# Scores of a split-precision attention: three products on 64 rows of a head, two heads side by side, where four on 128 rows stood

## The chip, the cores and the metric

The kernel runs on one core of a Trainium2 chip (trn2). The metric is the device time of one execution in microseconds (us), the median of several runs. TensorE (PE) multiplies, with weight loads (PEld) as instructions of their own; VectorE (DVE), ScalarE (ACT) and GpSimd (POOL) work on rows of 128 partitions; SyncE (SP) issues nearly all DMAs.

## The reference

Attention over 8 batches of 8 heads, with queries averaged in pairs, and then a feed-forward part over all tokens (float32, head dimension 64, 1152 keys, 576 pooled queries a head):

```python
q_pool = q.reshape(B, H, S // factor, factor, D).mean(axis=3)      # B, H, S, D = 8, 8, 1152, 64; factor 2
scores = scale * np.matmul(q_pool, k.transpose(0, 1, 3, 2))
scores = scores - np.max(scores, axis=-1, keepdims=True)
attn = np.exp(scores)
attn = attn / (np.sum(attn, axis=-1, keepdims=True) + 1e-09)
out = np.matmul(attn, v)                                           # heads side by side make x: 4608 x 512
h = np.maximum(np.maximum(x @ w1, x @ w2), x @ w3)                 # 4608 x 768
return h @ w_out                                                   # 4608 x 512
```

## The kernel before, in words

Two heads make a pair, whose 2 x 64 head dimensions fill the 128 partitions. The attention runs in 64 turns `d`, each for one pair and one half of its queries (288 columns, `QH`). In a turn there are nine blocks `kk` of 128 keys. For each block PE writes the scores of both heads into one of two PSUM slots (`pqk`, a bank for each head), ACT copies them to SBUF (`s`, L664), and DVE keeps the running maximum (`acc`, L670 and L673). A slot is free for the block after next when both have read it. Then comes the maximum over all keys: DVE folds (L714), PE turns (L724), DVE and ACT take a high and a low part, POOL spreads them (`diag`, L739), PE makes them wide (L790). DVE subtracts (L809), ACT takes the exponential (L815), POOL adds the keys up (`ksum`, L846 and L848), PE multiplies by the values (`pav`, L875) and totals the sums (L891), and the quotient becomes `xr` (L902), split into `xh` and `xl` for the feed-forward part. That part (`ffn`) is done in chunks of up to 512 tokens, three products for each product of two split operands (L1165 and L1221), and its matmuls stand between those of the attention on PE.

The first pairs (`n < PLAIN`, `plain_heads`) take the scores in plain float32: L642, one matmul a head on 64 rows, the two heads at rows 0 and 64 of the array. A matmul in plain float32 is two records in the trace. The other pairs (`heads`) use numbers of type float32r: q and k are cut into a high part (a cast on ACT, L528 and L535) and a low part (a subtraction on POOL, L532 and L539), in tiles `qraw` and `kraw`. Then DMAs on SP (`move_q` L573, `move_k` L565) put the parts where 128 rows of one head hold both: `kc` has the high part of k on rows 0 to 63 and the low part on rows 64 to 127, and `qq` has each part of q twice. Four matmuls of 128 rows make a block: for each head one with the high part of q (L654) and one with its low part (L655).

The order of all work is written out: `ORDER` lists the steps of the plan by number, and every engine and every DMA queue works them off in that order. `mode`, `cols` and the times in the steps were for the program that made the list; at run time they do nothing.

Of the kernel before, what the change touches and what calls it, by code (L numbers as in the profile page):

```python
# [8 lines left out]
F32 = mybir.dt.float32  # L9
# [10 lines left out]
NK = 9  # L20
# [301 lines left out]
THIRDS = 7  # L322
LENT = 4
SUMS = range(8)
SPLIT = 8
AHEAD = {3: 5, 4: 5, 5: 5, 6: 5, 7: 5}
GIFT = {0: 1, 1: 2, 2: 3, 3: 3, 4: 1}
PLAIN = 10
APART = 0

class Step:
    def __init__(self, plan, engines, fn, after, **kw):
# [970 lines left out]
```

## Time and profile before

| | |
|---|---|
| time, median of 3 runs (lowest to highest) | 1349.48 us (1347.28 to 1354.3) |
| span of the profiled execution, first to last instruction | 1345.0 us |
| TensorE clock granted over the span, share of full | 0.999 |
| busy share of the span: PE, PEld, DVE, ACT, POOL | 98%, 77%, 75%, 68%, 83% |
| matmul records | 8544 |

The time of the profiled execution by itself is not given beside its span; the span lies 4.5 us under the median of the runs. PE's busy share counts a matmul from its start to its end, and matmuls overlap, so the starts of successive matmuls tell the pace, not the durations. The last 145 us are feed-forward work alone, with the other engines nearly idle.

### The profile page before, as it was taken

What the parts mean: (1) busy time and instruction counts of PE and PEld (TensorE: products, weight loads), DVE (VectorE), ACT (ScalarE), POOL (GpSimd) and SP (SyncE); (2) the same over time, 40 slices, a digit from 0 to 9 for tenths busy, and PEclk for the clock granted to TensorE, in tenths of its full rate; (3) what the DMA queues carried; (4) which work ended last, traced back from release to release, by engine and by line L of the source; (5) the groups of instructions that cost most, each with busy time, mean ns of one, the idle gap of its engine ahead of it and who ended that gap; (6) DMA issues with size and microseconds to landing.
All of it is one profiled execution on the core that took longest, in us unless ns stands there. A gap on an engine that the chain in (4) does not pass through costs nothing.

```text
span 1345.0 us, 24149 instructions
## 1 busy us (share of the span) xinstructions
PE 1322.0 (98%) x8544; PEld 1029.4 (77%) x8544; DVE 1015.1 (75%) x1351; ACT 907.9 (68%) x1547; POOL 1123.0 (83%) x895
## 2 busy tenths in 40 slices
PE   7999999999999999999999999999999999999999
PEld 3455668887777877777777877777777877779998
DVE  7889987888779878887888888878888888842110
ACT  6998886776667766786677766776767766652211
POOL 3797899999899999999899999898999998865310
PEclk9999999999999999999999999999999999999999
DMA  6677787875676467547676557656675576527341
GB/s 220 236 266 244 250 243 236 242 239 161 173 214 177 127 191 230 153 136 213 175 217 184 154 150 222 167 162 194 167 201 159 164 201 172 159 71 227 133 160 49
DMA packets 112296, 250.11 MB, mean 186 GB/s; under 512 B 14512, under 2 KB 68272, under 8 KB 112176
## 3 DMA queue, kind: packets, MB, share of 16 engines
q1 hardware_dynamic: 112176, 248.57, 62.6%
q8 instruction: 68, 1.11, 0.4%
q14 instruction: 52, 0.43, 0.1%
HBM read 168.30 MB, written 18.87 MB: 139 GB/s over the span
## 4 chain that ended last, share of the span: by engine, by line
PE 83%; POOL 5%; DVE 4%; DMA 4%; issue 2%; ACT 2%; SPq 0%; ACTq 0%; POOLq 0%; DVEq 0%
PE ff L1165 31%; PE pav L875 16%; PE ff L1221 10%; PE pqk L654 8%; PE pqk L655 8%; PE pqk L642 3%; POOL ksum L848 3%; PE ff L891 2%; PE ff L875 2%; DMA kc<-kraw 2%; DVE acc L673 2%; PE bank_a L790 1%; PE ff L924 1%; DMA w<-w_split 1%; ACT s L664 1%
## 5 line engine op out<-in xcount | busy, mean ns | idle before, releaser
L848 POOL TENSOR_TENSOR ksum<-ksum,s 128x576 f32<-128x576 f32 x407 | 580.7, 1427 | 26.5 <-ACT s L815 8.8
L1165 PE MATMUL ff<-xh,w 128*128 128x512 f32 (+2 forms) x1584 | 470.3, 355 | 2.0 <-DMA w<-w_split 1.7
L664 ACT COPY s<-pqk 128x576 f32<-128x576 f32 x576 | 359.7, 641 | 142.3 <-PE pqk L655 100.3
L673 DVE TENSOR_TENSOR acc<-acc,pqk 128x576 f32<-128x576 f32 x448 | 334.7, 747 | 62.0 <-ACT s L664 52.3
L815 ACT ACTIVATE s<-s 128x864 f32<-128x864 f32 x384 | 348.0, 931 | 18.1 <-DVE s L809 17.2
L1165 PEld LDWEIGHTS ff<-xh,w 128*128 128x128 f32 x1584 | 283.9, 188 | 38.6 <-issue 4.5
L1165 PE MATMUL ff<-xl,w 128*128 128x512 f32 (+2 forms) x792 | 279.7, 353 | 0.0
L654 PE MATMUL pqk<-qq,kc 128*128 128x288 f32 x936 | 263.5, 300 | 4.4 <-DVE acc L673 1.2
L655 PE MATMUL pqk<-qq,kc 128*128 128x288 f32 x936 | 259.5, 295 | 0.0
L875 PE MATMUL pav<-s,v 128*64 128x288 f32 x2016 | 254.6, 407 | 0.0
L809 DVE TENSOR_TENSOR s<-s,bank_a 128x864 f32<-128x864 f32 x192 | 199.0, 1047 | 45.1 <-PE bank_a L790 38.0
L875 PEld LDWEIGHTS pav<-s,v 128*64 128x64 f32 x2016 | 144.2, 137 | 98.9 <-PE pqk L655 1.5
L654 PEld LDWEIGHTS pqk<-qq,kc 128*128 128x128 f32 x936 | 175.7, 188 | 30.0 <-DVE acc L673 8.9
L809 DVE TENSOR_TENSOR s<-s,pmb 128x864 f32<-128x864 f32 x182 | 188.8, 1045 | 1.2 <-PE pmb L790 1.0
L655 PEld LDWEIGHTS pqk<-qq,kc 128*128 128x128 f32 x936 | 176.0, 188 | 10.6
L1221 PE MATMUL ff<-h,wo 128*128 128x512 f32 (+2 forms) x792 | 162.7, 352 | 0.0
L1165 PEld LDWEIGHTS ff<-xl,w 128*128 128x128 f32 x792 | 148.9, 188 | 9.4
L1186 DVE TENSOR_TENSOR hm<-hm,ff 128x512 f32<-128x512 f32 (+2 forms) x132 | 76.3, 578 | 101.9 <-PE ff L1165 97.9
L1221 PEld LDWEIGHTS ff<-h,wo 128*128 128x128 f32 x792 | 129.0, 188 | 13.6 <-issue 0.9
L1197 POOL TENSOR_TENSOR h<-hm,h 128x512 fp32r<-128x512 f32 (+2 forms) x66 | 71.8, 1088 | 71.9 <-ACT h L1194 71.7
L899 DVE RECIPROCAL rs<-rs 128x288 f32<-128x288 f32 (+1 forms) x64 | 110.6, 1728 | 9.6 <-ACT rs L895 7.8
L846 POOL TENSOR_TENSOR ksum<-s 128x576 f32<-128x576 f32 x61 | 87.5, 1435 | 23.0 <-ACT s L815 22.6
(70 smaller groups left out, 1228.9 us busy)
## 6 DMA issues: line engine op xcount, KB each, us to landing
w<-w_split SPq DMA_DIRECT2D x180, 512.0 KB, 4.7
kc<-kraw SPq DMA_DIRECT2D x312, 96.0 KB, 3.6
qq<-qraw SPq DMA_DIRECT2D x208, 144.0 KB, 3.9
v<-in_vr_dram SPq DMA_DIRECT2D x36, 576.0 KB, 5.5
qraw<-in_qT_dram SPq DMA_DIRECT2D x26, 576.0 KB, 4.3
kraw<-in_kT_dram SPq DMA_DIRECT2D x26, 576.0 KB, 5.0
w<-in_win_dram SPq DMA_DIRECT2D x18, 512.0 KB, 4.3
w_split<-wo SPq DMA_DIRECT2D x18, 512.0 KB, 6.9
```

The source lines that it names most:

```text
L654: nc.tensor.matmul(ps[:, h - hs[0], :QH], w, qq[:, 0, h], start=True, stop=False)
L655: nc.tensor.matmul(ps[:, h - hs[0], :QH], w, qq[:, 1, h], start=False, stop=True)
L664: nc.scalar.copy(o.s[kk // 3][:, kk % 3, slice(*hs)], o.ps[kk, hs][:, :, :QH])
L673: nc.vector.tensor_tensor(acc, acc, ps, op=ALU.max)
L809: nc.vector.tensor_tensor(s, s, o.pb[h][:, None, :w].broadcast_to([P, 3, w]), op=ALU.subtract)
L815: nc.scalar.activation(s, s, AF.Exp, scale=SCALE)
L846: vec[e].tensor_tensor(o.ksum, o.s[0][:, 0], x, op=ALU.add)
L848: vec[e].tensor_tensor(o.ksum, o.ksum, x, op=ALU.add)
L875: nc.tensor.matmul(o.pav[64 * h : 64 * h + 64, :QH], pr.v[:, kk, h], o.s[kk // 3][:, kk % 3, h], start=(kk == 0), stop=(kk == NK - 1),)
L899: nc.vector.reciprocal(o.rs, o.rs)
L1165: nc.tensor.matmul(t.ps[:, : hi - lo], w[:, a, kk], xx[:, kk, lo:hi], start=(kk == 0 and i == 0), stop=(kk == 3 and i == 2),)
L1221: nc.tensor.matmul(t.ps[:, : hi - lo], ww[:, kk, ms], hh[kk // 3][:, kk % 3, lo:hi], start=(kk == 0 and i == 0), stop=(kk == 5 and i == 2),)
```

## The change

Pairs from `n = 8` on (`PLAIN` was 10) are split, 28 pairs in place of 26. The parts of q and k stay on the rows on which they were loaded: ACT casts the high part straight into `qq` and `kc`, POOL subtracts the low part into them, in pieces of 288 and 384 columns, and the DMAs `move_q` and `move_k` are gone. A block of scores is now six matmuls: high x high, high x low, low x high (the product of the two low parts is left out), each for both heads, one head on rows 0 to 63 and one on rows 64 to 127 of the array. `qq` is half as large and has three buffers (`QBUFS`). `ORDER` is made anew.

```diff
-PLAIN = 10
+PLAIN = 8
+QBUFS = 3
...
-        def k_high(e, x, y):
-            nc.scalar.copy(o.hl[:, 0, x:y].bitcast(F32R), o.hl[:, 1, x:y])
-        def k_low(e, x, y):
-            lo = o.hl[:, 1, x:y]
-            vec[e].tensor_tensor(lo.bitcast(F32R), lo, o.hl[:, 0, x:y], op=ALU.subtract)
...
-        def move_k(e, c, h, part):
...
-            nc.sync.dma_start(
-                o.kc[c][64 * part : 64 * part + 64, h].bitcast(F32),
-                o.hl[64 * h : 64 * h + 64, part, KC * c : KC * c + KC],
-            )
...
+        def q_high(e, half):
+            o.qq[half] = qpool.tile([P, 2, QH], F32R, tag="qq", name=f"qq{n}_{half}")
+            nc.scalar.copy(o.qq[half][:, 0], o.qr[:, 1, QH * half : QH * half + QH])
+        def q_low(e, half):
+            src = o.qr[:, 1, QH * half : QH * half + QH]
+            nc.gpsimd.tensor_tensor(o.qq[half][:, 1], src, o.qq[half][:, 0], op=ALU.subtract)
+        def k_high(e, c):
+            o.kc[c] = kpool.tile([P, 2, KC], F32R, tag="kc", name=f"kc{n}_{c}")
+            nc.scalar.copy(o.kc[c][:, 0], o.kr[:, KC * c : KC * c + KC])
+        def k_low(e, c):
+            src = o.kr[:, KC * c : KC * c + KC]
+            nc.gpsimd.tensor_tensor(o.kc[c][:, 1], src, o.kc[c][:, 0], op=ALU.subtract)
...
                     kc, qq = pr.kc[kk // 3], pr.qq[o.half]
-                    for h in range(*hs):
-                        w = kc[:, h, kk % 3 * P : kk % 3 * P + P]
-                        nc.tensor.matmul(ps[:, h - hs[0], :QH], w, qq[:, 0, h], start=True, stop=False)
-                        nc.tensor.matmul(ps[:, h - hs[0], :QH], w, qq[:, 1, h], start=False, stop=True)
+                    for i, (x, y) in enumerate(((0, 0), (0, 1), (1, 0))):
+                        for h in range(2):
+                            r = slice(64 * h, 64 * h + 64)
+                            nc.tensor.matmul(
+                                ps[:, h, :QH],
+                                kc[r, x, kk % 3 * P : kk % 3 * P + P],
+                                qq[r, y],
+                                start=i == 0,
+                                stop=i == 2,
+                                tile_position=(64 * h, 0),
+                            )
```

In the changed kernel the lines have other numbers: the six score matmuls are L582, the feed-forward ones L1099 and L1155, the values L809, `diag` made wide L724, the low parts of k and q L524 and L516 on POOL, and the key sums L782.

How the order moves is shown at two places. The first is PE in turn 33, behind the values of turn 32 (`pav32`), where the scores of pair 21 begin. Before, two blocks of scores go straight on to the widening of turn 33's maximum (`bank_a`, L790) and to feed-forward work:

```order
L875 MATMUL pav32_6030<-s32_2_5780,v20_5532 64x288 x6
L654 MATMUL pqk1_127<-qq21_0_5818,kc21_1_5918 128x288
L655 MATMUL pqk1_127<-qq21_0_5818,kc21_1_5918 128x288
L654 MATMUL pqk1_127<-qq21_0_5818,kc21_1_5918 128x288
L655 MATMUL pqk1_127<-qq21_0_5818,kc21_1_5918 128x288
L654 MATMUL pqk0_126<-qq21_0_5818,kc21_1_5918 128x288
L655 MATMUL pqk0_126<-qq21_0_5818,kc21_1_5918 128x288
L654 MATMUL pqk0_126<-qq21_0_5818,kc21_1_5918 128x288
L655 MATMUL pqk0_126<-qq21_0_5818,kc21_1_5918 128x288
L790 MATMUL bank_a_94<-diag1_116,wide_108 128x288
L1165 MATMUL ff0_130<-xh_120,w0_122 128x512
```

The changed kernel at the same place, with two blocks of six, then six feed-forward matmuls, the first widening, and the next block:

```order
L809 MATMUL pav32_6424<-s32_2_6147,v20_6324 64x288 x6
L582 MATMUL pqk0_126<-qq21_0_6306,kc21_0_6313 128x288 x6
L582 MATMUL pqk1_127<-qq21_0_6306,kc21_1_6369 128x288 x6
L1099 MATMUL ff1_131<-xh_120,w0_122 128x512
L1099 MATMUL ff1_131<-xl_121,w0_122 128x512
L1099 MATMUL ff1_131<-xh_120,w0_122 128x512 x2
L1099 MATMUL ff1_131<-xl_121,w0_122 128x512
L1099 MATMUL ff1_131<-xh_120,w0_122 128x512
L724 MATMUL pmb33_1_6487<-diag1_116,wide_108 128x288
L582 MATMUL pqk0_126<-qq21_0_6306,kc21_1_6369 128x288 x6
```

The scores keep coming two blocks at a time between values and feed-forward work, but each such group is now of another tile shape than what stands on either side of it. Over the whole order PE goes from one tile shape (128 rows x 128 columns, 64 x 128, 128 x 64 and the like) to another 260 times before and 695 times now.

The second place is POOL, where the low parts of pair 21 are made. Before, one instruction of 1152 columns makes the low part of k, between the key sums of turns 30 and 31 (that of q, in 576 columns, stands four rows above this piece):

```order
L848 TENSOR_TENSOR ksum30_5616<-ksum30_5616,s30_2_5419 128x576
L1017 TENSOR_TENSOR xl_121<-xr_119,xh_120 128x96
L848 TENSOR_TENSOR ksum30_5616<-ksum30_5616,s30_2_5419 128x576 x2
L539 TENSOR_TENSOR kraw21_5650<-kraw21_5650 128x1152
L846 TENSOR_TENSOR ksum31_5830<-s31_0_5469 128x576
L1017 TENSOR_TENSOR xl_121<-xr_119,xh_120 128x128
L739 TENSOR_TENSOR diag0_115<-pick_110,parts0_113 64x576
```

In the changed kernel the pieces of k and q stand apart, here among the sums of turn 32, on both sides of `diag`:

```order
L524 TENSOR_TENSOR kc21_1_6369<-kraw21_6310,kc21_1_6369 128x384
L836 TENSOR_TENSOR xr_119<-xr_119,rs31_6420 128x288
L951 TENSOR_TENSOR xl_121<-xr_119,xh_120 128x96
L951 TENSOR_TENSOR xl_121<-xr_119,xh_120 128x128
L673 TENSOR_TENSOR diag1_116<-pick_110,parts1_114 64x576
L524 TENSOR_TENSOR kc21_2_6471<-kraw21_6310,kc21_2_6471 128x384
L782 TENSOR_TENSOR ksum32_6380<-ksum32_6380,s32_1_6097 128x576
L516 TENSOR_TENSOR qq21_1_6316<-qraw21_6103,qq21_1_6316 128x288
```

The low parts moved later by about a turn, no DMA stands between them and PE any more, and POOL has five instructions for a pair's low parts where it had two.

## Rows read from the trace of the kernel before

**Rows 1.** The page: span, busy time by engine, and the chain that ended last.

```profile
span 1345.0 us, 24149 instructions
PE 1322.0 (98%) x8544; PEld 1029.4 (77%) x8544; DVE 1015.1 (75%) x1351; ACT 907.9 (68%) x1547; POOL 1123.0 (83%) x895
PE 83%; POOL 5%; DVE 4%; DMA 4%; issue 2%; ACT 2%; SPq 0%; ACTq 0%; POOLq 0%; DVEq 0%
```

**Rows 2.** PE's waits from 205 us to the end: us in total, times, longest.

```profile
PE pqk L654 <- DVE acc L673: 1.2, 2, 0.6
PE pqk L654 <- DMA kc<-kraw: 1.2, 2, 0.6
```

**Rows 3.** By stage: us; busy us of PE, PEld, DVE, ACT, POOL; clock; DMA share.

```profile
100.00:205.00 105.00, 102.83 (x773) 67.65 (x763) 95.34 (x144) 89.68 (x152) 91.39 (x77) 1.00 0.79 244
700.00:800.00 100.00, 100.00 (x622) 77.69 (x619) 81.60 (x102) 71.11 (x124) 96.96 (x79) 1.00 0.59 168
205.00:1125.00 920.00, 915.66 (x5758) 722.68 (x5757) 753.97 (x956) 653.97 (x1100) 857.50 (x667) 1.00 0.66 186
```

**Rows 4.** Groups by line and shape: count, then busy us and mean ns.

```profile
L654 PE MATMUL pqk<-qq,kc 128*128 128x288 f32 x936 | 263.5, 300 | 4.4 <-DVE acc L673 1.2 <-DMA kc<-kraw 1.2 <-DMA w<-w_split 1.1
```

**Rows 5.** PE's timeline, two blocks of split scores: start us, us, instruction.

```profile
608.00 0.29 PE L654 MATMUL pqk<-qq,kc 128*128 128x288 f32 x1
608.12 0.29 PE L655 MATMUL pqk<-qq,kc 128*128 128x288 f32 x1
...
608.91 0.30 PE L655 MATMUL pqk<-qq,kc 128*128 128x288 f32 x1
```

**Rows 6.** Timelines: four plain score matmuls, and four of their weight loads.

```profile
64.91 0.65 PE L642 MATMUL pqk<-qq,kc 64*128 64x288 f32 x4
...
60.25 0.30 PEld L642 LDWEIGHTS pqk<-qq,kc 64*128 64x128 f32 x4 [0.51 <-DVE acc L673]
```

**Rows 7.** PE's timeline where the tile shape changes, one way and back.

```profile
139.75 0.29 PE L1165 MATMUL ff<-xh,w 128*128 128x288 f32 x1
139.98 0.51 PE L642 MATMUL pqk<-qq,kc 64*128 64x288 f32 x2
...
173.68 0.65 PE L642 MATMUL pqk<-qq,kc 64*128 64x288 f32 x4
174.26 0.40 PE L1165 MATMUL ff<-xh,w 128*128 128x288 f32 x1
```

**Rows 8.** Groups by line and shape on POOL and ACT, columns as in rows 4.

```profile
L539 POOL TENSOR_TENSOR kraw<-kraw 128x1152 fp32r<-128x1152 f32 x26 | 69.9, 2688 | 7.2 <-DMA w<-w_split 3.3 <-ACT kraw L535 2.8 <-DMA qraw<-in_qT_dram 1.1
L532 POOL TENSOR_TENSOR qraw<-qraw 128x576 fp32r<-128x576 f32 x26 | 37.1, 1425 | 1.5 <-ACT qraw L528 1.3 <-DMA v<-in_vr_dram 0.2
L1197 POOL TENSOR_TENSOR h<-hm,h 128x288 fp32r<-128x288 f32 x24 | 19.4, 808 | 55.3 <-ACT h L1194 55.3
L528 ACT CAST qraw<-qraw 128x576 fp32r<-128x576 f32 x26 | 17.6, 676 | 1.7 <-POOL qraw L525 1.6
L1197 POOL TENSOR_TENSOR h<-hm,h 128x384 fp32r<-128x384 f32 x6 | 6.1, 1009 | 8.3 <-ACT h L1194 8.2
```

**Rows 9.** DMA issues: name, queue, count, KB each, median us to landing.

```profile
kc<-kraw SPq DMA_DIRECT2D x312, 96.0 KB, 3.6
qq<-qraw SPq DMA_DIRECT2D x208, 144.0 KB, 3.9
```

**Rows 10.** Groups by line: the two readers of a score slot.

```profile
L664 ACT COPY s<-pqk 128x576 f32<-128x576 f32 x576 | 359.7, 641 | 142.3 <-PE pqk L655 100.3 <-PE pqk L642 17.4 <-POOL ksum L848 8.6
L673 DVE TENSOR_TENSOR acc<-acc,pqk 128x576 f32<-128x576 f32 x448 | 334.7, 747 | 62.0 <-ACT s L664 52.3
```

**Rows 11.** PE's timeline: one plain score pair, then key sums, four tiles side by side.

```profile
61.67 0.41 PE L642 MATMUL pqk<-qq,kc 64*128 64x288 f32 x2
62.01 2.62 PE L924 MATMUL ff<-s,ones 128*32 128x288 f32 x36
```

**Rows 12.** POOL's `diag`, one a turn, in the long stage: busy us (count).

```profile
205.00:1125.00 920.00, 56.39 (x49) 1.00 0.66 186
```

More of the change, by code (lines that the diff above doesn't have):

```diff
@@ L382, in tile_attention_ffn @@
     kpool = ctx.enter_context(tc.tile_pool(name="kpool", bufs=4))
-    qpool = ctx.enter_context(tc.tile_pool(name="qpool", bufs=2))
+    qpool = ctx.enter_context(tc.tile_pool(name="qpool", bufs=QBUFS))
     vpool = ctx.enter_context(tc.tile_pool(name="vpool", bufs=2))
@@ L465, in load_q @@
         def load_q(e, half):
-            o.q[half] = qpool.tile([P, 2, 2, QH], F32R, tag="qq", name=f"qq{n}_{half}")[:, :, 0].bitcast(F32)
+            o.q[half] = qpool.tile([P, 2, QH], F32R, tag="qq", name=f"qq{n}_{half}").bitcast(F32)
             nc.sync.dma_start(o.q[half], qT[b, j, :, :, QH * half : QH * half + QH])
@@ L477, in plain_heads @@
         for i, (d, half) in enumerate(todo):
-            x = step("load", d, [("sp", 0.5)], lambda e, half=half: load_q(e, half), [qk.get((d - 2, NK - 1))], size=288)
+            x = step("load", d, [("sp", 0.5)], lambda e, half=half: load_q(e, half), [qk.get((d - QBUFS, NK - 1))], size=288)
             o.qready[half] = [step("prep", d, [dve(QH) if d == 0 else pool(QH)], lambda e, half=half: qsum(e, half), [x])]
@@ L504, in heads, with load_k, load_q @@
             before = None
-        first = n == 0
-        kparts = [(KC * c, KC * c + KC) for c in range(3)] if first else [(0, NK * P)]
-        qparts = [(0, QH), (QH, NQ)] if first else [(0, NQ)]
-        def load_k(e, x, y):
-            if x == 0:
-                o.hl = raw.tile([P, 2, NK * P], F32, tag="kraw", name=f"kraw{n}")
-            nc.sync.dma_start(o.hl[:, 1, x:y], kT[b, j, :, x:y])
-        def load_q(e, x, y):
-            if x == 0:
-                o.q = raw.tile([P, 2, NQ], F32, tag="qraw", name=f"qraw{n}")
-            nc.sync.dma_start(o.q[:, :, x:y], qT[b, j, :, :, x:y])
+        def load_k(e):
+            o.kr = raw.tile([P, NK * P], F32, tag="kraw", name=f"kraw{n}")
+            nc.sync.dma_start(o.kr, kT[b, j])
+        def load_q(e):
+            o.qr = raw.tile([P, 2, NQ], F32, tag="qraw", name=f"qraw{n}")
+            nc.sync.dma_start(o.qr, qT[b, j])
         def load_v(e):
@@ L521, in load_v @@
             nc.sync.dma_start(o.v, v[b, j])
-        def qsum(e, x, y):
-            lo = o.q[:, 1, x:y]
-            vec[e].tensor_tensor(lo, o.q[:, 0, x:y], lo, op=ALU.add)
-        def q_high(e, x, y):
-            nc.scalar.copy(o.q[:, 0, x:y].bitcast(F32R), o.q[:, 1, x:y])
-        def q_low(e, x, y):
-            lo = o.q[:, 1, x:y]
-            vec[e].tensor_tensor(lo.bitcast(F32R), lo, o.q[:, 0, x:y], op=ALU.subtract)
-        def k_high(e, x, y):
-            nc.scalar.copy(o.hl[:, 0, x:y].bitcast(F32R), o.hl[:, 1, x:y])
@@ L537, in k_low @@
-        def k_low(e, x, y):
-            lo = o.hl[:, 1, x:y]
-            vec[e].tensor_tensor(lo.bitcast(F32R), lo, o.hl[:, 0, x:y], op=ALU.subtract)
-        def pieces(key, at, engines, fn, parts, after, size=0):
-            return [
-                step(key, at + 0.01 * i, engines(y - x), lambda e, x=x, y=y: fn(e, x, y), a, size=(y - x) * size)
-                for i, ((x, y), a) in enumerate(zip(parts, after))
-            ]
-        work = (lambda m: [dve(m)]) if first else (lambda m: [pool(m)])
@@ L548, in heads @@
-        cast = lambda m: [("act", 0.09 + m / 1200)]
-        sp = lambda m: [("sp", 0.5)]
-        lq = pieces("load", r, sp, load_q, qparts, [before.qmoved if before else []] * len(qparts), size=1)
-        lk = pieces("load", r, sp, load_k, kparts, [before.kmoved if before else []] * len(kparts), size=0.5)
-        x = pieces("prep", r, work, qsum, qparts, [[a] for a in lq])
-        x = pieces("prep", r, cast, q_high, qparts, [[a] for a in x])
-        qs = pieces("prep", r, work, q_low, qparts, [[a] for a in x])
@@ L555, in heads @@
-        x = pieces("prep", r, cast, k_high, kparts, [[a] for a in lk])
-        ks = pieces("prep", r, work, k_low, kparts, [[a] for a in x])
-        o.kc, o.qq = {}, {}
-        o.kready, o.qready, o.kmoved, o.qmoved = {}, {}, [], []
-        def move_k(e, c, h, part):
-            if c not in o.kc:
-                o.kc[c] = kpool.tile([P, 2, KC], F32R, tag="kc", name=f"kc{n}_{c}")
-            nc.sync.dma_start(
-                o.kc[c][64 * part : 64 * part + 64, h].bitcast(F32),
-                o.hl[64 * h : 64 * h + 64, part, KC * c : KC * c + KC],
-            )
@@ L570, in move_q @@
-        def move_q(e, half, h, to):
-            if half not in o.qq:
-                o.qq[half] = qpool.tile([P, 2, 2, QH], F32R, tag="qq", name=f"qq{n}_{half}")
-            (nc.scalar if e == "act" else nc.sync).dma_start(
-                o.qq[half][64 * to : 64 * to + 64, :, h].bitcast(F32),
-                o.q[64 * h : 64 * h + 64, :, QH * half : QH * half + QH],
-            )
-        for d, half in todo:
-            o.qready[half] = [
-                step(
-                    "move",
-                    d,
-                    [("act" if first and half == 0 else "sp", 0.6)],
-                    lambda e, half=half, h=h, to=to: move_q(e, half, h, to),
-                    [qs[half % len(qs)], qk.get((d - 2, NK - 1))],
-                    size=144,
-                )
-                for h in range(2)
-                for to in range(2)
-            ]
-            o.qmoved += o.qready[half]
-            if d == r:
-                for c in range(3):
-                    gone = qk[kuse[-4]] if len(kuse) > 3 else None
-                    kuse.append((o.last, 3 * c + 2))
-                    o.kready[c] = [
-                        step(
-                            "move",
-                            r + 0.1 * (c + 1),
-                            [("sp", 0.6)],
-                            lambda e, c=c, h=h, part=part: move_k(e, c, h, part),
-                            [ks[c % len(ks)], gone],
-                            size=96,
-                        )
-                        for h in range(2)
-                        for part in range(2)
-                    ]
-                    o.kmoved += o.kready[c]
@@ L609, in heads, with qsum @@
-        o.lv = step(
-            "load",
-            r + 2,
-            sp(0),
-            load_v,
-            [av[pairs[n - 2].last]] if n > 1 else [] if n else o.qready[0] + o.kmoved,
-            size=576,
-        )
+        def qsum(e):
+            nc.gpsimd.tensor_tensor(o.qr[:, 1], o.qr[:, 0], o.qr[:, 1], op=ALU.add)
+        o.kc, o.qq = {}, {}
+        o.kready, o.qready = {}, {}
+        def q_high(e, half):
+            o.qq[half] = qpool.tile([P, 2, QH], F32R, tag="qq", name=f"qq{n}_{half}")
+            nc.scalar.copy(o.qq[half][:, 0], o.qr[:, 1, QH * half : QH * half + QH])
@@ new lines, in heads @@
+        cast = lambda m: [("act", 0.09 + m / 1200)]
+        lq = step("load", r, [("sp", 0.5)], load_q, before.qsplit if before else [], size=576)
+        lk = step("load", r, [("sp", 0.5)], load_k, before.ksplit if before else [], size=576)
+        sq = step("prep", r, [pool(NQ)], qsum, [lq])
+        o.qsplit, o.ksplit = [], []
+        for d, half in todo:
+            gone = [qk.get((d - QBUFS, NK - 1))]
+            x = step("prep", d, cast(QH), lambda e, half=half: q_high(e, half), [sq] + gone)
+            y = step("prep", d, [pool(QH)], lambda e, half=half: q_low(e, half), [x])
+            o.qready[half] = [x, y]
+            o.qsplit += [x, y]
@@ L619, in tile_attention_ffn @@
+        for c in range(3):
+            gone = qk[kuse[-4]] if len(kuse) > 3 else None
+            kuse.append((o.last, 3 * c + 2))
+            x = step("prep", r, cast(KC), lambda e, c=c: k_high(e, c), [lk, gone])
+            y = step("prep", r, [pool(KC)], lambda e, c=c: k_low(e, c), [x])
+            o.kready[c] = [x, y]
+            o.ksplit += [x, y]
+        o.lv = step("load", r + 2, [("sp", 0.5)], load_v, [av[pairs[n - 2].last]], size=576)
     blanks = step("top", max(TURN - 4, 0), [("dve", 3.2)], lambda e: blank(), [])
@@ L679, in scores @@
                     r,
-                    [pe(250 * n if pr.plain else 266 * n)],
+                    [pe(250 * n if pr.plain else 200 * n)],
                     product,
@@ L683, in scores @@
                     cols=576 * n,
-                    mode=3 if pr.plain else 0,
+                    mode=3,
                     take="ff" if apart else None,
```

545 rows, old and new, of the table ORDER are left out of this document.

## The prediction

> **What bounds the kernel now.** I read the page first: PE is busy for 98% of the span and has 83% of the chain that ended last, POOL 83% of the span and 5% of the chain [rows 1]. Then PE's waits: from 205 us to the end no line of them is over 1.2 us [rows 2], so PE is fed all the time, and what counts there is how closely its instructions follow each other. Then the stages, since a mean over the span hides the second engine: from 205 to 1125 us PE is busy for 915.7 of 920 us, and POOL for 857.5, which is 93.2%; its best stretch of 100 us has 96.96, with PE still at 100.00 [rows 3]. DVE (82%) and ACT (71%) have room there [rows 3]. The reader is to see that PE decides, and that POOL stands close behind it, where the span's 83% does not show it.
>
> **The sum on PE.** Durations of matmuls overlap, so I take starts.
>
> Removed: 1872 matmuls of split scores, 468 blocks of four (L654 has 936 [rows 4], L655 as many). In a run of eight the first starts at 608.00 and the last at 608.91 [rows 5]: 0.91 / 7 = 0.130 us each, and 1872 x 0.130 = 243.4 us. Pairs 8 and 9 leave the plain form: 2 pairs x 2 turns x 9 = 36 blocks. A plain block is two records for each head. Four records, which is one block, take 0.65 us from the first start to the last end [rows 6], and two side by side take 0.41 [rows 11]; so a pair of heads follows the other after 0.24 us, a block costs 0.48, and 36 of them 17.3 us.
>
> Added: 28 pairs x 2 turns x 9 = 504 blocks of three pairs of matmuls, one matmul for each head, 1512 in all. No float32r matmul on 64 rows is in the trace. From below, the plain pair needs 0.24 us for two passes over the same 288 columns, so one pass is 0.12; from above, two matmuls one behind the other take 0.26. I take 0.130, the pace of one float32r matmul of 288 columns, because the plain records show that two heads on 64 rows share their time: two take 0.41, which is barely longer than the 0.40 of one [rows 7, 11]. 1512 x 0.130 = 196.6 us (181 at the lower end, 393 at the upper). Issue is no obstacle: 36 matmuls and their 36 loads pass in 2.62 us [rows 11], at most 36 ns for each instruction, and a pair of scores needs four in 130 ns.
>
> Moved: the scores now have another tile shape than the feed-forward matmuls around them. In the trace that is not free. From L1165 to L642 the starts are 139.75 and 139.98, 0.23 apart in place of 0.13; on the way back the second pair of the run starts at 173.68 + 0.24 = 173.92 and L1165 at 174.26, 0.34 later in place of 0.24 [rows 7]. Each change of shape costs about 0.10 from rounded starts; I take 0.095. The order has 695 changes in place of 260, 435 more, and 435 x 0.095 = 41.3 us. Ends: 0.09 and 0.10 (39 to 44 us).
>
> Together: -243.4 - 17.3 + 196.6 + 41.3 = -22.8 us. Of the 64 us that the products save, the shape changes take back two thirds.
>
> **The term for POOL.** The low parts cost a pair 2.688 + 1.425 = 4.11 us now; in pieces they cost 3 x 1.009 + 2 x 0.808 = 4.64 (rows of the same shapes and types in the feed-forward part) [rows 8], so 0.53 more. Pairs 8 and 9 bring 4.64 us and a sum of about 1.43 in place of two of 0.81, 4.5 us each on POOL, in the stage from 100 to 205 us, where it has 91.4 of 105 busy [rows 3]; that fits into its gaps. In the long stage there are 49 turns [rows 12], 24.5 pairs and 441 blocks: PE loses 441 x 0.130 = 57.3 us, gets 49/56 of the 435 changes, 381 x 0.095 = 36.2, and needs 920 - 21.1 = 899 us. POOL needs 857.5 + 24.5 x 0.53 = 870.5, which is 96.8% of 899. That is what it reached in its best 100 us, and it would have to hold it for the whole stage. Between the mean of 93.2% and the best of 96.96% I take 96%, nearer to the best, since PE did not wait in that stretch: 870.5 / 0.96 = 907 us, 8 us over what PE needs. What is late then is `diag`, which stands in POOL's order among key sums and low parts; PE's widening of the maximum waits for it, and with it all feed-forward matmuls behind it, and next DVE's subtractions and ACT's exponentials.
>
> **What I cost at nothing.** The 520 DMAs for `kc` and `qq` go [rows 9], and SP's queue is free for the weights sooner; PE's waits for `kc` in the long stage were 1.2 us [rows 2], so little can be gained, and at most a few us in all. The wait of the scores is now on POOL and ACT themselves, without 3.6 to 3.9 us of landing [rows 9], and the order uses that up by making the low parts about a turn later; if POOL is late by more than what is left, the score matmuls stop and the feed-forward ones queued behind them too. ACT has three casts more a pair, each shorter than the 0.676 us of a cast of 576 columns [rows 8]: under 2 us a pair beside some 11 us of idle time (266 us in the stage [rows 3] over 24.5 pairs). Without that cover, the copy of 0.641 us and the maximum of 0.747 [rows 10] would let go of a score slot later and PE would wait for it. Both orders put two blocks side by side and then other work, so the slots are asked for no more often than before. The third buffer of `qq` only lets its casts go earlier.
>
> **A rule that speaks against it.** Two score matmuls share their time only if their weight loads do. Four loads on 64 rows take 0.30 us from the first start to the last end [rows 6]; at the 0.130 us at which loads and matmuls of the whole array follow each other [rows 5], the fourth would not even start before 0.39. So they do overlap. The Trainium skill, TensorE: Matmul & The Clock Gate, section LDWEIGHTS, says that a load is priced by its columns and not by its rows, 128 / 1.2 GHz = 107 ns for these. An estimate by that page, with the six loads of a block one behind the other: 504 x 6 x 0.107 = 323 us in place of 197, and about 1455 us in all. Four loads in 0.30 us speak against that reading.
>
> **The rivals.**
> - *POOL holds the pace.* If it is busy for no more than 93.2% of the stage, as now, the stage takes 870.5 / 0.932 = 934 us, 35 over PE's 899, and the kernel 1349.5 - 22.8 + 35 = 1362 us: slower. It decides from 94.2% down, where the stage takes 924 and the gain is gone. For it: POOL's idle time is spread over waits that come from the loop of maximum, `diag` and exponential, and some of that stays however late POOL is. Against it: the stretch at 96.96%.
> - *POOL keeps up, and a pair goes at less than 0.130.* With no POOL term 1349.5 - 22.8 = 1327; with 0.12 a pair another 15 us less, 1312, but then POOL would have to be busy for over 98% of the stage, which no stretch shows.
> - *The heads do not go side by side in float32r* (the change does not do what it says): six matmuls, or six loads, one behind the other at 0.130 make 393 us in place of 197, and 1327 + 197 = 1524. The plain records speak against it, but they are of another type.
>
> **How the numbers follow.** The span of the profiled execution is 1345.0 us [rows 1], 4.5 under the median of the runs; I leave that difference as it is. 1349.5 - 22.8 + 8 = 1334.7, rounded to 1335 us. Chances: this forecast (1325 to 1343) 0.54; POOL no hindrance or a faster pair (1310 to 1325) 0.17; POOL holding back (1343 to 1362) 0.20, of it three quarters within half a per cent of now; heads one behind the other 0.05; something else that costs, such as an order that fits badly, 0.04. Half a per cent, 1342.7 to 1356, is about what a measurement of this kernel can tell. So faster 0.72, same 0.15, slower 0.13. The range of 1312 to 1354 leaves out the serial case, the worst of POOL and the tip of the fast case.
>
> **What would show it.** Score matmuls in pairs that start a few ns apart, pair after pair 0.13 us later; 0.22 to 0.24 us from a feed-forward matmul of 288 columns to the first score; POOL at 95 to 97% of the long stage; PE's waits on `diag` and on the low parts some 10 us where they were near nothing. I am wrong if pairs start 0.26 apart, if a change of shape costs twice or nothing between float32r matmuls, or if POOL's busy share stays at 93% and PE waits for it.

## The result: slower by 1.2%

The changed kernel takes 1364.25 us (1363.83 to 1366.44, 4 runs), the kernel before in the same comparison 1348.38 us (1343.78 to 1354.3, 4 runs): a ratio of 1.0121, 95% interval 1.0093 to 1.0149. The forecast was 1335 us and faster. The span of the profiled execution is 17.1 us longer than the one before, 1362.1 against 1345.0 [rows 1].

The page of the changed kernel, as [rows 1] has it of the one before: the span, the busy time of the engines, and the chain.

```profile
span 1362.1 us, 25330 instructions
PE 1344.8 (99%) x9552; PEld 972.3 (71%) x9552; DVE 1023.7 (75%) x1351; ACT 915.0 (67%) x1635; POOL 1139.8 (84%) x981
PE 85%; DVE 2%; POOL 1%; issue 1%; DMA 0%; ACT 0%; DVEq 0%; POOLq 0%; ACTq 0%
```

PE is the bound as before, and more so: POOL's part of the chain fell from 5% to 1%, that of the DMAs from 4% to 0%. The long stage of the changed kernel, with the columns of [rows 3], and below it POOL's `diag` in the same stage, as in [rows 12]:

```profile
205.00:1125.00 920.00, 919.44 (x6523) 653.30 (x6524) 747.29 (x941) 648.76 (x1159) 856.47 (x733) 1.00 0.34 119
...
205.00:1125.00 920.00, 55.25 (x48) 1.00 0.34 119
```

In 920 us the kernel gets through 48 turns where it got through 49. PE is busy for 919.4 of them, POOL for 856.5, 93.1% (857.5 before), and the DMA share fell from 0.66 to 0.34. PE's waits from 205 us to the end are all here (us in total, times, longest):

```profile
PE bank_a L724 <- POOL diag L673: 0.2, 1, 0.2
PE pqk L582 <- DVE acc L607: 0.2, 1, 0.2
```

So hardly any wait of PE is left; its own instructions follow each other more slowly. TensorE's granted clock is no cause: it is 1.00 of the full 2.4 GHz in this stage in both kernels [rows 3]. Where the time goes is seen in PE's timeline, here a stretch between two runs of scores (start us, us, instruction):

```profile
599.84 0.85 PE L1155 MATMUL ff<-h,wo 128*128 128x512 f32 x3
600.62 1.06 PE L582 MATMUL pqk<-qq,kc 64*128 64x288 f32 x12
601.60 2.35 PE L1155 MATMUL ff<-h,wo 128*128 128x512 f32 x9
603.88 0.40 PE L582 MATMUL pqk<-qq,kc 64*128 64x288 f32 x2
```

Two blocks of scores, six pairs of matmuls, take 0.98 us from their first start to the start of what follows. Before, two blocks were eight matmuls at 0.130, 1.04 us [rows 5]. That 0.06 us is all that a run of two blocks gains, though six pairs at 0.13 are only 0.78 us; and the nine feed-forward matmuls behind it pay as well, with 2.28 us from 601.60 to 603.88 where nine at 0.23 take 2.07. Single records of the same stretch show how:

```profile
600.29 0.40 PE L1155 MATMUL ff<-h,wo 128*128 128x512 f32 x1
600.62 0.40 PE L582 MATMUL pqk<-qq,kc 64*128 64x288 f32 x2
...
600.85 0.42 PE L582 MATMUL pqk<-qq,kc 64*128 64x288 f32 x4
...
601.25 0.42 PE L582 MATMUL pqk<-qq,kc 64*128 64x288 f32 x4
...
601.60 0.50 PE L1155 MATMUL ff<-h,wo 128*128 128x512 f32 x1
...
601.94 0.40 PE L1155 MATMUL ff<-h,wo 128*128 128x512 f32 x1
```

Inside a run the heads go side by side and pair follows pair at 0.13 us: two pairs last 0.42 from the first start to the last end, which is 0.13 and the 0.29 of one. At the edges there are two losses, not one. From the last feed-forward matmul to the first pair it is 0.33 us in place of the 0.23 of such a matmul: that is the 0.10 I had priced. And from the first pair to the second it is 600.85 - 600.62 = 0.23 in place of 0.13, and from the first feed-forward matmul to the second 601.94 - 601.60 = 0.34 in place of 0.23. The first matmul of the new shape is 0.10 us longer (0.40 where later pairs have 0.29, 0.50 where later ones have 0.40). A change of shape costs 0.2 us, twice its price in the prediction.

### The profile page after: what moved, and what is told of

Its sections match the earlier page's. It is cut to its first block, busy times and chain, and to the rows that moved or that the text cites. A ratio compares the mean times of both kernels' runs of the same rounds, so it can differ in the third digit from the quotient of the medians.

```text
span 1362.1 us, 25330 instructions
## 1 busy us (share of the span) xinstructions
PE 1344.8 (99%) x9552; PEld 972.3 (71%) x9552; DVE 1023.7 (75%) x1351; ACT 915.0 (67%) x1635; POOL 1139.8 (84%) x981
## 4 chain that ended last, share of the span: by engine, by line
PE 85%; DVE 2%; POOL 1%; issue 1%; DMA 0%; ACT 0%; DVEq 0%; POOLq 0%; ACTq 0%
PE ff L1099 34%; PE pqk L582 17%; PE pav L809 17%; PE ff L1155 11%; PE ff L825 3%; PE bank_a L724 1%; PE pmb L724 1%; DVE s L743 1%; DVE acc L607 1%; PE bank_a L658 1%; POOL ksum L782 0%; DMA w<-in_wout_dram 0%; DVE w L1017 0%; DVE w L1012 0%; POOL ksum L780 0%
## 5 line engine op out<-in xcount | busy, mean ns | idle before, releaser
L782 POOL TENSOR_TENSOR ksum<-ksum,s 128x576 f32<-128x576 f32 x407 | 579.7, 1425 | 21.8 <-ACT s L749 5.1
L1099 PE MATMUL ff<-xh,w 128*128 128x512 f32 (+2 forms) x1584 | 473.3, 364 | 0.7 <-DVE xr L895 0.7
L598 ACT COPY s<-pqk 128x576 f32<-128x576 f32 x576 | 352.7, 640 | 164.8 <-PE pqk L582 121.6
L749 ACT ACTIVATE s<-s 128x864 f32<-128x864 f32 x384 | 346.0, 932 | 15.9 <-DVE s L743 15.0
L1099 PEld LDWEIGHTS ff<-xh,w 128*128 128x128 f32 x1584 | 283.6, 188 | 58.4 <-issue 23.5
L1099 PE MATMUL ff<-xl,w 128*128 128x512 f32 (+2 forms) x792 | 280.7, 354 | 0.0
L582 PE MATMUL pqk<-qq,kc 64*128 64x288 f32 x3024 | 276.5, 312 | 0.9 <-DVE acc L607 0.7
L582 PEld LDWEIGHTS pqk<-qq,kc 64*128 64x128 f32 x3024 | 210.0, 185 | 88.2 <-issue 51.8
L809 PE MATMUL pav<-s,v 128*64 128x288 f32 x2016 | 254.5, 407 | 0.0
L809 PEld LDWEIGHTS pav<-s,v 128*64 128x64 f32 x2016 | 143.8, 137 | 99.0 <-issue 0.3
L1155 PE MATMUL ff<-h,wo 128*128 128x512 f32 (+2 forms) x792 | 164.2, 358 | 0.0
L1099 PEld LDWEIGHTS ff<-xl,w 128*128 128x128 f32 x792 | 149.2, 188 | 11.8
L1155 PEld LDWEIGHTS ff<-h,wo 128*128 128x128 f32 x792 | 128.8, 188 | 21.6 <-issue 7.1
L833 DVE RECIPROCAL rs<-rs 128x288 f32<-128x288 f32 (+1 forms) x64 | 110.6, 1729 | 26.4 <-ACT rs L829 22.8
L673 POOL TENSOR_TENSOR diag<-pick,parts 64x576 fp32r<-64x576 f32 x64 | 73.7, 1151 | 25.6 <-DVE parts L670 24.3
L524 POOL TENSOR_TENSOR kc<-kraw,kc 128x384 fp32r<-128x384 f32 x84 | 85.0, 1016 | 1.8 <-ACT kc L520 1.8
```

What stands on the lines that cost most here:

```text
L524: nc.gpsimd.tensor_tensor(o.kc[c][:, 1], src, o.kc[c][:, 0], op=ALU.subtract)
L582: nc.tensor.matmul(ps[:, h, :QH], kc[r, x, kk % 3 * P : kk % 3 * P + P], qq[r, y], start=i == 0, stop=i == 2, tile_position=(64 * h, 0),)
L598: nc.scalar.copy(o.s[kk // 3][:, kk % 3, slice(*hs)], o.ps[kk, hs][:, :, :QH])
L749: nc.scalar.activation(s, s, AF.Exp, scale=SCALE)
L782: vec[e].tensor_tensor(o.ksum, o.ksum, x, op=ALU.add)
L809: nc.tensor.matmul(o.pav[64 * h : 64 * h + 64, :QH], pr.v[:, kk, h], o.s[kk // 3][:, kk % 3, h], start=(kk == 0), stop=(kk == NK - 1),)
```

## The experiments

Theory A says that, and that it explains the result alone: 435 changes more at about 0.19 us, against 64 us of score matmuls saved. Theory B keeps 0.095 a change and looks for the loss in the new order or in POOL's pieces; theory C has it wholly outside the changes of shape. Each experiment but the last edits the score matmuls of the changed kernel, and all leave its order alone.

**Fewer changes of shape, the scores as long: three matmuls on all rows.** It mixes the two heads, so it does not compute the scores.

```diff
-                    for i, (x, y) in enumerate(((0, 0), (0, 1), (1, 0))):
...
+                    w = lambda x: kc[:, x, kk % 3 * P : kk % 3 * P + P]
+                    nc.tensor.matmul(ps[:, 0, :QH], w(0), qq[:, 0], start=True, stop=True)
+                    nc.tensor.matmul(ps[:, 1, :QH], w(0), qq[:, 1], start=True, stop=False)
+                    nc.tensor.matmul(ps[:, 1, :QH], w(1), qq[:, 0], start=False, stop=True)
```

> The changed kernel, but a block of scores is three matmuls on all 128 rows in place of three pairs on 64 (it mixes the two heads, so the scores are others). The pace of the scores stays at 3 x 0.13 us a block, and the order has 229 changes of tile shape in place of 695. Theory A (a change costs PE about 0.2 us, 0.09 before the first matmul of the new shape and 0.10 before its second): PE has 466 x 0.195 = 91 us less to do, so 1273 us if nothing else binds, and up to some 1320 if POOL, at 93% of the long stage now, becomes the bound. Theory B (a change costs the 0.095 us of the prediction, and the rest of the loss is the new order or the POOL pieces): 44 us less, 1320 us with PE still without waits. Theory C (the loss is not in the changes of shape at all): within 1% of 1364.

Measured: 1335.65 us, 0.9915 of before (0.9898 to 0.9932), some 29 us under the changed kernel. C falls. The time lies above the 1320 us of both A (up to which it let other engines bind) and B, and B had PE without waits there. The stage and PE's longest waits in it from 205 us on tell why:

```profile
205.00:1125.00 920.00, 896.96 (x5371) 672.93 (x5371) 763.76 (x968) 665.64 (x1187) 878.85 (x752) 1.00 0.36 124
...
PE bank_a L651 <- DVE crest L641: 9.5, 25, 1.2
PE pqk L580 <- DVE acc L600: 7.1, 33, 0.4
PE bank_a L717 <- POOL diag L666: 2.3, 6, 0.5
```

PE is idle for 23 of 920 us now, and in the listed waits it waits for DVE, for the fold of the maximum and for the maximum that frees a score slot, far more than for POOL. POOL stands at 878.9, 95.5%. So this run frees PE of more than the other engines can follow: with two thirds of the changes of shape gone and three products a block, it ends only 11 us under the kernel before. Whether this order allows more was not tried.

**Fewer changes, the scores as many as before: four matmuls on all rows.** The same edit with a fourth product, again mixing the heads.

```diff
+                    for h in range(2):
+                        nc.tensor.matmul(ps[:, h, :QH], w(0), qq[:, h], start=True, stop=False)
+                        nc.tensor.matmul(ps[:, h, :QH], w(1), qq[:, h], start=False, stop=True)
```

> The changed kernel, but a block is four matmuls on all 128 rows, as many as before the change (it mixes the heads, so the scores are others). Against the changed kernel it has 466 changes of shape fewer and 504 x 0.132 = 66 us more of score matmuls. Theory A (0.195 us a change): 1364 - 91 + 66 = 1339 us, near the kernel before and without its DMAs and order. Theory B (0.095 a change): 1364 - 44 + 66 = 1386. Theory C (the order or the rest of the change costs the time): 1364 + 66 = 1430 if the changes cost nothing.

Measured: 1353.24 us, 1.0046 of before (1.0029 to 1.0063). It has 66 us more of score matmuls than the changed kernel and is 11 us faster. That is outside B and C; by A, 0.195 a change, it should have been 14 us faster still. Per change the difference gives (66.5 + 11) / 466 = 0.17 us. PE's listed waits have grown to little over 1 us only. A part of the rest is in pauses too short for that list, since records of 0.29 us overlap at a pace of 0.13: inside its runs of scores 70 steps are longer than 0.15 us, 7.5 us over the pace in all (21 steps and 2.4 us in the changed kernel, 16 and 3.2 us in the one before). Where the remainder went is not shown. New order, POOL's pieces and missing DMAs together are no large loss: with four matmuls on 128 rows the kernel is within half a per cent of the one before.

**More changes, a small matmul as the means.** Two runs put a matmul of 64 columns ahead of each block, which the block then overwrites: once on rows 0 to 63, the scores' own shape, once on all rows.

```diff
+                    w = kc[:64, 0, kk % 3 * P : kk % 3 * P + P]       # all rows: kc[:, 0, ...], qq[:, 0, :64]
+                    nc.tensor.matmul(ps[:, 0, :64], w, qq[:64, 0, :64], start=True, stop=True, tile_position=(0, 0))
```

> The changed kernel with one more matmul of 64 columns ahead of each block of scores, on rows 0 to 63, so of the scores' own tile shape; its result is overwritten. 504 matmuls more and no change of shape more: all theories expect the price of the 504 themselves, 0.03 to 0.13 us each, 1379 to 1430 us. It is the base for the next one.

> The same small matmul ahead of each block, but on all 128 rows: the order then has 1185 changes of shape in place of 695. Against the run with the small matmul in the scores' own shape, theory A (0.195 us a change) expects 490 x 0.195 = 96 us more, theory B (0.095) 47 us, theory C (changes cost nothing) 0.

Measured: 1414.05 and 1471.57 us, 57.5 apart, 0.117 a change: nearer to B than to A. But the base was not a clean one. The small matmul in the scores' own shape cost 50 us / 504 = 0.10 each although its columns pass in far less: the records of one run with it show that.

```profile
600.27 0.29 PE L580 MATMUL pqk<-qq,kc 64*128 64x64 f32 x1
600.28 0.79 PE L584 MATMUL pqk<-qq,kc 64*128 64x288 f32 x7
600.89 0.19 PE L580 MATMUL pqk<-qq,kc 64*128 64x64 f32 x1
600.91 0.64 PE L584 MATMUL pqk<-qq,kc 64*128 64x288 f32 x5
601.48 0.50 PE L1101 MATMUL ff<-xh,w 128*128 128x512 f32 x1
```

The score matmul behind the second small one starts after 0.02 us, yet the run of two blocks takes 1.21 us in place of 0.98. A matmul this short seems too short to load the next weights behind, and it also holds up one head of the pair; so both runs carry a cost of the means, not equal in the two, and their difference decides nothing.

**More changes, a matmul as long as the others as the means.** The same test with 288 columns: a fourth pair side by side, or one matmul on all rows.

```diff
+                    w = kc[:, 0, kk % 3 * P : kk % 3 * P + P]         # all rows: 490 changes more
+                    nc.tensor.matmul(ps[:, 0, :QH], w, qq[:, 0], start=True, stop=True)
...
+                    for h in range(2):                                # or a fourth pair: no change more
+                        r = slice(64 * h, 64 * h + 64)
+                        w = kc[r, 0, kk % 3 * P : kk % 3 * P + P]
+                        nc.tensor.matmul(ps[:, h, :QH], w, qq[r, 0], start=True, stop=True, tile_position=(64 * h, 0))
```

> The changed kernel with a fourth pair of matmuls ahead of each block, as long as the others (288 columns, 64 rows, the two heads side by side), overwritten by the block. 504 pairs more at 0.131 us are 66 us, no change of tile shape more: all theories 1430 us. If two heads on 64 rows did not run side by side, it would be 132 us, 1496. It is the base for the next one.

> The changed kernel with one more matmul of 288 columns on all 128 rows ahead of each block, overwritten by it: the same 504 x 0.131 = 66 us of streaming as the run with a fourth pair, and 490 changes of tile shape more (1185 in place of 695). Long enough that the next weights load behind it, unlike the small matmul of the first runs. Against the run with the fourth pair, theory A (0.195 us a change) expects 96 us more, about 1526 us in all; theory B (0.095) 47 us; theory C 0.

Measured: 1428.41 us with the pair (ratio 1.0603, 1.0576 to 1.0631) and 1519.40 us with the matmul on all rows (1.1280, 1.1255 to 1.1305). The pair costs (1428.41 - 1365.08) / 504 = 0.126 us against the changed kernel on the same chip (below), so two heads do go side by side in float32r. The two runs are 91.0 us apart, and 91.0 / 490 = 0.186 us a change: A, twice B's price. The timeline of the run with more changes shows it at one place:

```profile
602.25 0.40 PE L580 MATMUL pqk<-qq,kc 128*128 128x288 f32 x1
602.57 0.66 PE L584 MATMUL pqk<-qq,kc 64*128 64x288 f32 x6
603.17 0.50 PE L1101 MATMUL ff<-xh,w 128*128 128x512 f32 x1
603.50 0.40 PE L1101 MATMUL ff<-xl,w 128*128 128x512 f32 x1
```

One matmul of 288 columns between two changes takes 0.32 us to the next start where 0.13 would do, three pairs take 0.60 in place of 0.39, and the feed-forward matmul behind them 0.33 in place of 0.23.

**Fewer changes in the kernel itself.** The widening of the maximum needs only 64 of its rows. Done on 64 rows at 39 places, it leaves out nothing and makes 34 changes of shape fewer.

```diff
+                if (d, h) in NARROW:
+                    nc.tensor.matmul(
+                        o.pb[h][:, :QH], wide[:64], half.rearrange("p t k -> p (t k)")[:64],
+                        start=True, stop=True, tile_position=(0, 0),
+                    )
+                    return
```

> The changed kernel with the widening of the maximum on 64 rows (the other 64 hold zeros) at the 39 places where it stands between a score block and a matmul of another shape than the whole array: same numbers, same count of matmuls, 34 changes of tile shape fewer, most of them where PE never waits. Theory A: 34 x 0.195 = 6.6 us less than the changed kernel on the same chip; theory B 3.2; theory C 0.

> The changed kernel once more, on the chip of the three runs beside it, as their base: 1364 us.

Measured: 1360.36 us (ratio 1.0097, 1.0075 to 1.0118) beside 1365.08 us of the changed kernel itself (1.0128, 1.0103 to 1.0154). The two ratios' intervals overlap, but the times themselves do not (1359.65 to 1361.61 us against 1364.12 to 1366.72), so fewer changes do help, and C, which expects nothing, falls here too. The 4.7 us lie between the 6.6 of A and the 3.2 of B and do not decide between them. It is the fastest form of the changed kernel that computes everything, and still slower than the kernel before.

## Why the prediction was wrong

The step that failed is the price of a change of shape in "The sum on PE": I took 0.095 us, from the start of the last matmul of one shape to the start of the first of the other, and the runs give 0.186. The second half of the cost lies behind that first matmul, and I looked only ahead of it. It could have been read from the rows that I showed: the first pair of L642 behind a change is 0.51 us long [rows 7], where a pair further on has 0.41 [rows 11], and the L1165 behind the other change is 0.40, where the L1165 ahead of the first has 0.29 [rows 7]. I even used that 0.40 as the length of one plain record; a quarter of it was the loss itself. (A single L642 record does take 0.40 us, so what I drew from it, that two heads share their time, stands.) A change that costs twice its price was among my own signs of being wrong, and it is the one that came. A record that is 0.10 us longer than its like was a loss of 0.10 us, in a timeline where durations otherwise overlap and say little. With 0.186 the sum of the prediction reads -243.4 - 17.3 + 196.6 + 435 x 0.186 = +16.8 us; the spans differ by 17.1 and the medians by 15.9. That it meets so closely is in part luck: by the same price the run with four matmuls should take 1344 us, and it took 1353; at the 0.17 which that run gives, the sum is +9.9.

The rest of it, point by point:

- *PE decides, from 205 us on.* Right, more than before: 99.9% of the long stage.
- *The pace of a pair, 0.130 us.* Right: 0.13 in the trace of the changed kernel, 0.126 by the run with a fourth pair. The rival that the heads go one behind the other is out, and with it the estimate that put the six loads of a block in a row: a pair with its two loads takes 0.13 us.
- *435 changes more.* Right as a count: the traces have 698 and 263. At 0.186 us they account for the whole of the loss.
- *The 8 us for POOL.* Wrong in this kernel: PE waits 0.2 us for `diag`, and POOL's share stayed at 93.1%, since PE became slower and not faster. I had named a share of 93% as a sign that I was wrong, together with waits of PE for POOL; the share came, the waits did not. The rival "POOL holds the pace" gave 1362 us, 2 us from the result, and its mechanism is out: a right number for a wrong reason. (Its break-even was also a little off: a gain of 22.8 us is gone at 899 + 22.8 = 922 us, a share of 94.4% and not 94.2%.) Where PE was made faster than in the prediction (three matmuls on all rows), the waits that came were mostly for DVE's maxima, with POOL at 95.5%. So the limit beside PE looks like that loop over several engines rather than POOL alone; which of its links is the tightest was not tried.
- *What I cost at nothing* (the DMAs, ACT's casts, the third buffer, the score slots) cost nothing that can be seen: the waits of PE are 0.4 us in the two lines above, and the longer steps inside its runs of scores are no dearer than before (2.4 us against 3.2).

## What to carry to other kernels

Price a change of matmul tile shape by both of its ends, before the first matmul of the new shape and before its second, and multiply it by the changes in the order, not by the edits in the code. Here a run of two blocks among feed-forward work saves 2 x 0.13 us of streaming and pays two changes, 0.37 us; by the same numbers a run would need three blocks between two changes only to come out even. With two PSUM slots the third would have to wait for the readers of the first (0.641 and 0.747 us [rows 10]); that was not tried. In a timeline of overlapping records, look for a record that is longer than its like: here each one marked a place where PE stood still while it counted as busy and no wait was listed.

## What the runs showed of the hardware

A change between tile shapes of float32r matmuls cost 0.186 us in 490 cases, about 0.09 to 0.10 us before the first matmul of the new shape and 0.10 more before its second. The Trainium skill, TensorEngine Tiling (Array Packing), section Key Properties, says that a change of tiling mode drains TensorE, without a price; the first part agrees with that. The second part is the time of a weight load that does not run behind the matmuls of the other shape. The loads have records of their own (their ends overlap as well, so starts count):

```profile
601.60 0.19 PEld L1155 LDWEIGHTS ff<-h,wo 128*128 128x128 f32 x1 [0.16 <-issue]
601.71 0.42 PEld L1155 LDWEIGHTS ff<-h,wo 128*128 128x128 f32 x2
```

Inside a run a load starts with the matmul ahead of it (in the kernel before, the load of L655 at 608.00 with the L654 of 608.00 [rows 5]). Behind the change the first load starts only with its own matmul, at 601.60, and the next 0.11 us later, so the second matmul follows that much later. The kernel before has such a record with no change of shape (L654, 0.38 where its like have 0.29), behind the turning of the maximum (L724). That matmul has 128 columns only, and the next one starts 0.03 us after it, while the loads of the two behind it start 0.11 us apart, at 600.53 and 600.64:

```profile
600.53 0.27 PE L724 MATMUL bank_a<-ident,crest 128*128 128x128 f32 x1
600.56 0.38 PE L654 MATMUL pqk<-qq,kc 128*128 128x288 f32 x1
600.77 0.29 PE L655 MATMUL pqk<-qq,kc 128*128 128x288 f32 x1
```

So a longer record marks a load that was not covered, and a change of shape is one way to get it. The Trainium skill, TensorE: Matmul & The Clock Gate, section LDWEIGHTS, prices a load by its columns, P / 1.2 ns for P of them; an estimate by it is 107 ns for 128 columns and 53 ns for 64. The trace agrees with both. For 128 columns it has the 0.10 to 0.11 above. For 64 columns it has the sums (L825) behind a change of shape in the changed kernel, on PE's timeline:

```profile
590.82 0.66 PE L582 MATMUL pqk<-qq,kc 64*128 64x288 f32 x6
591.40 0.71 PE L825 MATMUL ff<-ksum,ones 128*64 128x288 f32 x4
591.94 4.53 PE L809 MATMUL pav<-s,v 128*64 128x288 f32 x36
```

Their two steps last 0.54 us to the start of the values, where two steps of 0.24 are 0.48: 0.06 more for a load of half the columns. That it is the load was read from the records and not tried by an edit of its own. A matmul of 64 columns ahead of each block cost 0.10 us each in the scores' own shape, nearly as much as one of 288 columns (0.126 a pair).
